# Transposes by DMA, V loads ahead of a weight load and another opening in a fused attention and mixture-of-experts kernel

## The chip, the cores and the metric

The kernel runs on one core of one Trainium2 chip. The metric is the device time of one execution in microseconds (us). The engines of a core work side by side, each through its own list of instructions in order: TensorE (PE) with its weight loads (PEld), VectorE (DVE), ScalarE (ACT), GpSimd (POOL) and SyncE (SP). Transfers are issued by SP, ACT and POOL and run on the core's 16 DMA engines.

## The reference

Attention over 32 global and 512 local tokens per batch (8 batches, 8 heads of 64), with a window of 32 to both sides for the local queries; its output is the input of a mixture of 8 experts, whose weights per token come from eight rounds of row and column scaling.

```python
out_g = sm(scale * q_g @ k_all.T) @ v_all                  # k_all = [k_g, k_l], v_all = [v_g, v_l]
s_ll  = where(|i - j| <= 32, scale * q_l @ k_l.T, -1e9)
out_l = sm([scale * q_l @ k_g.T, s_ll]) @ v_all
x = [out_g, out_l] as (B * S, H * D)                       # 4352 x 512
P = exp(x @ w_gate - max)
for _ in range(8):
    P /= P.sum(1) + 1e-9;  P /= P.sum(0) + 1e-9;  P *= N / E
out = sum over e of P[:, e] * (relu(x @ w1[e]) @ w2[e])    # w1: 512 x 1024, w2: 1024 x 512
```

## The kernel before

**Units and steps.** The attention has 32 units, n = 4b + hp: a batch b and a pair of heads hp. A loop over steps s = 0 to 33 (L453) is written out by hand, and every engine and queue keeps the written order. Step s makes the scores and probabilities of unit s and the output of unit s - 1, and does pieces of experts 0 and 1 for tokens that are ready:

- `st_A` transposes q and k of unit s + 1 on PE.
- `st_B` (in three parts, 3 + 3 + 2 blocks of 64 queries): scores on PE (L279, L281), the masked minimum on DVE (L286), exp on ACT into Pu (L289). A block of Pu is 128 local columns and 32 global ones.
- `st_D1` (unit s - 1): DVE copies the 32 global columns of all blocks to Pl (L295); PE transposes the 128 local columns of the 8 blocks (L298); DVE copies the result to pw (L300).
- `st_D2`: PE transposes xn of unit s - 2, the finished output, in four pieces (L308), and Pl of unit s - 1 (L312); ACT copies the two results to xT (L316) and to pg (L314).
- `st_E` (unit s - 1, at the end of step s): the output, from pw with va and vb (local keys) and pg with vgz (global keys), into po (L332); DVE divides into xn (L336, L337).
- `st_G1` to `st_G4`: the global queries, over the same k and V.
- `p_l1` and `p_l2` (L415, L429), called as `f1` and `f2`: four and two pieces a step of the two matrix products of experts 0 and 1, in between the parts above. They read xT, of the batch whose four units are complete. Their results go to memory (yd) by SP (L436).

Pu, pw and xn have two buffers each.

**V.** The local keys of a block of 64 queries are 128 rows that begin 32 rows before it. va holds V shifted by 32 rows, for the even blocks, and vb the rows 64 later, for the odd ones. `load_v` gives the steps of a batch's load: `first` (vg16, the global V rounded to half precision in memory, and 96 rows of va), three times `mid` (128 rows of va each) and `last`: POOL loads the final 32 rows of vb (L165), and then SP copies the rest of vb from va (L166, L167, L168) and, from batch 2 on, loads vgz from vg16 in four pieces (`load_vz`, L150).

**POOL's queue.** POOL issues every load that changes from single to half precision. At the head of a step the next entries of `queue` are taken (L466 to L474): for step 8 and later, two of the next batch's q and k loads in each of the steps hp = 0 and 1, three of its V steps at hp = 2, the rest at hp = 3. Then, in steps 8 to 31, POOL prepares weight sums that experts 2 to 7 use later (L476 to L478): an even step issues the load of a matrix (`sums_load`, tile pw, 1024 KB in half precision), the next step waits for it and forms four sums of 2.1 us each (`sums_form`, L113) and stores them (kept, L114). This tile pw has the name of the attention's pw and is another one. The V load of a batch b + 1 stands in the steps 4b + 2 and 4b + 3; its first use is the output of unit 4b + 4, in step 4b + 5.

**The opening.** Before the loop q and k of the first unit come by SP and ACT in single precision and are rounded on the core; step 0 also rounds and transposes the global q of batches 0 to 3 (`cast_g`, `transpose_g`). Steps 0 to 4 hold no expert work.

**After the loop** come the rest of experts 0 and 1 around the eight scalings (`tail`), and then experts 2 to 7 (class `Slot` and class `Unit`), from about 400 us to the end. Nothing there is edited.

Of the kernel before, what the change touches and what calls it, by code (L numbers as in the profile page):

```python
# [10 lines left out]
FP16 = mybir.dt.float16  # L11
FP32 = mybir.dt.float32
# [11 lines left out]
def kernel(  # L24
# [13 lines left out]
    nc = tc.nc  # L38

    B, H, Sl, Dh = q_l.shape  # L40
# [3 lines left out]
    P = 128  # L44
# [4 lines left out]
    NHB = Sl // HB  # L49
# [70 lines left out]
    with ExitStack() as att:  # L120
# [31 lines left out]
        def load_v(b):  # L152
            va, vb = vab[b % 2]
            vz = vgz[b % 2]
            src = v_l[b].rearrange("h s d -> s h d")

            def first():
                nc.gpsimd.dma_start(out=vg16[b], in_=v_g[b].rearrange("h g d -> g h d"))
                nc.gpsimd.dma_start(out=va[W:P, 0, :, 0:Dh], in_=src[0:96])

            def mid(j):
                nc.gpsimd.dma_start(out=va[:, j, :, 0:Dh], in_=src[P * j - W : P * j + 96])

            def last():
                nc.gpsimd.dma_start(out=vb[HB : HB + W, NJ - 1, :, 0:Dh], in_=src[Sl - W : Sl])  # L165
                nc.sync.dma_start(out=vb[96:P, NJ - 1], in_=va[W : 2 * W, 0])  # L166
                nc.sync.dma_start(out=vb[0:HB, :], in_=va[HB:P, :])  # L167
                nc.sync.dma_start(out=vb[HB:P, 0 : NJ - 1], in_=va[0:HB, 1:NJ])  # L168
                if b > 1:
                    load_vz(b)  # L170

            return [first] + [lambda j=j: mid(j) for j in range(1, NJ)] + [last]

        gst = {}

# [14 lines left out]
        def cast_g(tg):  # L190
            t, fv = gst[(0, tg)]
            nc.vector.tensor_copy(out=t, in_=fv)
            gst[(0, tg)] = t
# [72 lines left out]
        def st_B(n, part):  # L266
            b, hp = divmod(n, HP)
            qb, kt = qbd[n % 2], kTe[n % 4]
            if part == 0:
                st[n] = dict(Pu=att_wk.tile([P, NHB, SW], FP16, tag="Pu", name="Pu"),  # L270
                             mx=att_wk.tile([P, NHB], FP32, tag="mx", name="mx"))
            d = st[n]
            i0 = 3 * part
            ni = min(3, NHB - i0)
            sc = ps_sc.tile([P, 512], FP32, tag="sc")
            ms = att_wk.tile([P, 3, SW], FP32, tag="ms")
            for ii in range(ni):
                i = i0 + ii
                nc.tensor.matmul(sc[:, SW * ii : SW * ii + KW], qb[:, i, :],  # L279
                                 kt[:, HB * i : HB * i + KW], start=True, stop=True)  # L280
                nc.tensor.matmul(sc[:, SW * ii + KW : SW * (ii + 1)], qb[:, i, :],  # L281
                                 kgT[:, hp, Sg * b : Sg * (b + 1)], start=True, stop=True)
            for ii in range(ni):
                i = i0 + ii
                mi = 0 if i == 0 else (2 if i == NHB - 1 else 1)
                nc.vector.tensor_tensor_reduce(  # L286
                    out=ms[:, ii, :], in0=sc[:, SW * ii : SW * (ii + 1)], in1=mask[:, mi, :],
                    scale=-scale, scalar=BIG, op0=ALU.add, op1=ALU.min, accum_out=d["mx"][:, i : i + 1])
                nc.scalar.activation(out=d["Pu"][:, i, :], in_=ms[:, ii, :], func=AF.Exp, scale=-1.0,  # L289
                                     bias=d["mx"][:, i : i + 1])  # L290

        def st_D1(n):
            d = st[n]
            d["Pl"] = att_wk.tile([P, NHB, Sg], FP16, tag="Pl", name="Pl")
            nc.vector.tensor_copy(out=d["Pl"], in_=d["Pu"][:, :, KW:SW])  # L295
            ptw = ps_tr.tile([P, NHB, P], FP16, tag="tr")
            for i in range(NHB):
                nc.tensor.transpose(ptw[:, i, :], d["Pu"][:, i, 0:KW], identity)  # L298
            d["pw"] = att_wk.tile([P, NHB, P], FP16, tag="pw", name="pw")
            nc.vector.tensor_copy(out=d["pw"], in_=ptw)  # L300

        def st_D2(n, n2):
            tgx = ps_tr.tile([P, 6, P], FP16, tag="tr")
            if n2 is not None:
                b, hp = divmod(n2, HP)
                xn = st[n2]["xn"]
                for j in range(NJ):
                    nc.tensor.transpose(tgx[:, 2 + j, :], xn[:, j, :], identity)  # L308
            if n is not None:
                d = st[n]  # L310
                for t in range(2):
                    nc.tensor.transpose(tgx[:, t, :], d["Pl"][:, 4 * t : 4 * t + 4, :], identity)  # L312
                d["pg"] = att_wk.tile([P, 2, P], FP16, tag="pg", name="pg")
                nc.scalar.copy(out=d["pg"], in_=tgx[:, 0:2, :])  # L314
            if n2 is not None:
                nc.scalar.copy(out=xT[:, hp, Sl * b : Sl * (b + 1)], in_=tgx[:, 2:6, :].rearrange("p j q -> p (j q)"))  # L316
                del st[n2]

        def st_E(n):
            b, hp = divmod(n, HP)  # L320
            d = st[n]
            vz = vgz[b % 2]
            d["xn"] = att_wk.tile([P, NJ, P], FP16, tag="xn", name="xn")
            po = ps_po.tile([P, NJ, 256], FP32, tag="po")
            for j in range(NJ):
                for a in range(2):
                    for first in (True, False):
                        for par in range(2):
                            i, h = 2 * j + par, 2 * hp + a
                            lhs, rhs = (d["pw"][:, i], vab[b % 2][par][:, j, h, :]) if first else \  # L330
                                (d["pg"][:, i // 4], vz[:, i % 4, h, :])
                            nc.tensor.matmul(po[HB * par : HB * (par + 1), j, VW * a : VW * (a + 1)],  # L332
                                             lhs[:, HB * a : HB * (a + 1)], rhs, start=first, stop=not first)
            pv = po[:, :, 0 : 2 * VW].rearrange("p j (a v) -> p j a v", a=2)
            rr = att_wk.tile([P, NJ, 2], FP32, tag="rr2", name="rr2")
            nc.vector.reciprocal(out=rr, in_=pv[:, :, :, Dh])  # L336
            nc.vector.tensor_tensor(out=d["xn"].rearrange("p j (a v) -> p j a v", a=2), in0=pv[:, :, :, 0:Dh],  # L337
                                    in1=rr.unsqueeze(3).to_broadcast([P, NJ, 2, Dh]), op=ALU.mult)

        gs = {}  # L340

# [96 lines left out]
        def load_first():  # L438
            wts[0] = [load_w1(0)]
            nc.gpsimd.dma_start(out=wg_sb, in_=moe_w_gate.rearrange("(dko dki) e -> dki dko e", dki=P))  # L440

        queue = []
        NU = B * HP
        for t in range(2):
# [8 lines left out]
        for s in range(NU + 2):  # L453
            b, hp = divmod(s, HP)
            if s < NU and b + 1 < B:
                if hp == 0:
                    queue = load_qk(b + 1, 0, 4, H)
                if hp == 2:
                    queue += load_v(b + 1)
                if s == 4:  # L460
                    queue += [lambda: wts.__setitem__(1, [load_w1(1)]), lambda: wts[0].append(load_w2(0))]
                if s == 5:
                    queue += [lambda: load_g(1, "kgs"), lambda: load_g(1, "qgs")]
                if s == 7:
                    queue += [lambda: wts[1].append(load_w2(1))]
                take = 0 if s == 0 else len(queue) if s < 8 else 2 if hp < 2 else 3 if hp == 2 else len(queue)  # L466
                if s == 1:
                    queue += [load_first]
                    take = len(queue)
                for i, f in enumerate(queue[:take]):  # L470
                    f()
                    if s == 2 and i == 0:
                        load_vz(1)
                queue = queue[take:]  # L474
# [15 lines left out]
            def f1(eng):  # L490
                nonlocal n1
                if n1 < len(l1):
                    if l1[n1]:
                        p_l1(*l1[n1], eng)
                    n1 += 1
# [15 lines left out]
                st_G1(*divmod((s - 2) // 2, 2))  # L511
            if 1 <= s <= NU:
                st_D1(s - 1)
            if s == 3:
                st_E(1)
            if g_odd:
# [3 lines left out]
                st_B(s, 1)  # L520
            if 1 <= s:
                st_D2(s - 1 if s <= NU else None, s - 2 if s >= 4 else 0 if s == 3 else None)
            if s == 4:
                st_D2(None, 1)
            if 7 <= s < NU:
                st_B(s, 1)
            f1("a")
            if s + 1 < NU and s < 7:
                st_A(s + 1)
            if s == 0:  # L530
                cast_g("qgs")
                transpose_g(0, "qgs")
            f1("v")
            if s < NU:
# [15 lines left out]
            if s == 18:  # L550
                st_G4(0)
            f1("a")
        logits(NJ * (B - 1), NJ)


# [445 lines left out]
```

## Time and profile before

| | |
|---|---|
| three runs | 1039.04, 1041.32, 1042.68 us; median 1041.32 |
| profiled execution | 1041.35 us, its span 1039.6 us |
| busy over the span | PE 997.0, DVE 760.7, ACT 654.7, POOL 260.9 us |
| 139 to 307 us | PE 153.9, ACT 125.9, DVE 88.6, POOL 91.4 us of 168; DMA engines 92% |
| 307 to 352 us, the end of the attention loop | PE 43.5 us of 45 |
| 352 us to the end | PE 680.0 us of 687.6 |
| 128x128 transposes of Pu on PE (L298) | 256, median 0.219 us from issue to modelled end |
| 128x128 transposes of xn on PE (L308) | 128, the same |
| copy of these to pw on DVE (L300), to xT on ACT (L316) | 32 of 0.683 us, 32 of 0.605 us |
| copy of Pl on DVE (L295) | 32; shortest 0.216, median 0.222, longest 2.155 us |
| DMA queue of POOL, of SP and ACT | 87.32 MB and 50.27 MB; 47.7% and 14.9% of the 16 engines' span |

The span is the profiled stretch on the core; the execution's time has 1.75 us more around it. Busy time of PE is the time with a matrix instruction in flight, not PE at its peak. The chain that ended last is followed back from the last instruction: each piece names what released the next. A line such as "PE po L332 <- DMA vb<-va: 12.0, 3, 5.6" in the table of waits says that PE, at line 332, waited for a transfer into vb, 12.0 us in total, three times, the longest 5.6. In a timeline the columns are start, duration, engine, line, operation, output and input, and in brackets the idle time before and what ended it.

### The profile page before, as it was taken

To read this page: it belongs to the slowest core of one execution; us is meant where nothing else is said; L and a number is where in the kernel's file an instruction comes from. 1 tells how busy PE (TensorE), PEld (TensorE's weight loads), DVE (VectorE), ACT (ScalarE), POOL (GpSimd) and SP (SyncE) were. 2 spreads that over 40 slices of the span, in tenths; PEclk is the share of its full clock that TensorE was granted. 3 is DMA by queue.
4 is the path that set the end of the run, shared out by engine and by line. 5 is a ranking of instruction groups with operands and counts; after the bars stand their busy time and mean duration, and the time that the engine had idled before them with its cause. 6 is when DMAs were issued, how large, how long until landed. Compare 5 with 4: busy or idle time off the path is not lost.

```text
span 1039.6 us, 21929 instructions
## 1 busy us (share of the span) xinstructions
PE 997.0 (96%) x8650; PEld 648.6 (62%) x8650; DVE 760.7 (73%) x1862; ACT 654.7 (63%) x1377; POOL 260.9 (25%) x280
## 2 busy tenths in 40 slices
PE   5899999997979999999999999999999999999997
PEld 3666556564545554666666666676767676676764
DVE  6765565654535273689999887898889999888785
ACT  6788888876756556775555555556775555555551
POOL 7335665646463322012011111111111111011000
PEclk9899999998989999999999999999999999999999
DMA  9999988889795658465463433356554433233043
GB/s 176 193 157 165 211 142 207 147 184 169 163 195 139 189 152 243 101 165 125 111 135 87 106 60 101 76 169 183 143 133 107 105 102 90 65 72 72 1 102 122
DMA packets 134376, 139.38 MB, mean 134 GB/s; under 512 B 54144, under 2 KB 107648, under 8 KB 130688
## 3 DMA queue, kind: packets, MB, share of 16 engines
q0 software_dynamic: 103776, 87.32, 47.7%
q1 hardware_dynamic: 29664, 50.27, 14.9%
q8 instruction: 67, 1.10, 0.4%
q10 hardware_dynamic: 832, 0.39, 0.1%
q14 instruction: 37, 0.30, 0.1%
HBM read 144.20 MB, written 39.58 MB: 177 GB/s over the span
## 4 chain that ended last, share of the span: by engine, by line
PE 80%; DMA 9%; POOL 5%; DVE 2%; issue 1%; ACT 1%; SPq 1%; POOLq 0%; ACTq 0%; DVEq 0%
PE z L728 29%; PE pa L823 17%; PE pb L823 8%; PE py L429 8%; PE ph L415 7%; DMA pw<-in_moe_w_dram 5%; PE pc L823 5%; POOL psum L113 3%; DMA va<-in_v_l_dram 3%; PE zp L794 1%; PE po L332 1%; DMA vb<-va 1%; PE pt L257 1%; PE sc L279 1%; PE ptw L298 1%
## 5 line engine op out<-in xcount | busy, mean ns | idle before, releaser
L728 PEld LDWEIGHTS <-hs 128*128 128x128 f16 x2264 | 220.7, 98 | 92.9 <-issue 1.1
L728 PE MATMUL z<-w2e,hs 128*128 128x256 f16 x1304 | 195.6, 273 | 0.9 <-DVE oy L762 0.9
L728 PE MATMUL z<-v,hs 128*128 128x256 f16 x960 | 144.0, 273 | 0.0
L429 PE MATMUL py<-w2e,hT 128*128 128x512 f16 x544 | 131.5, 387 | 0.3 <-DVE lg L404 0.3
L415 PE MATMUL ph<-xT,w1e 128*128 128x512 f16 (+1 forms) x576 | 129.9, 368 | 1.8 <-DVE lg L404 1.4
L749 ACT COPY z<-z 128x256 f32<-128x256 f32 x98 | 35.0, 357 | 141.7 <-PE z L728 141.7
L823 PEld LDWEIGHTS <-w1e 128*128 128x128 f16 x960 | 86.6, 97 | 59.1 <-issue 2.5
L286 DVE CUSTOM_DVE_ANT_0 ms<-sc,mask 128x160 f32<-128x160 f32 x256 | 69.9, 320 | 69.8 <-PE sc L281 65.5
L823 PE MATMUL pa<-t,s 128*128 128x512 f16 x384 | 114.2, 379 | 0.3 <-ACT s L848 0.3
L289 ACT ACTIVATE Pu<-ms,mx 128x160 f16<-128x160 f32 x256 | 92.2, 424 | 20.5 <-DVE mx L286 18.4
L762 DVE SCALAR_TENSOR_TENSOR oy<-z,lg,oy 128x512 f32<-128x512 f32 x128 | 95.8, 749 | 7.3 <-ACT oy L767 5.1
L724 DVE TENSOR_TENSOR hs<-hs 128x512 f16<-128x512 f16 x224 | 94.8, 423 | 8.2
L827 DVE CUSTOM_DVE_ANT_0 hx<-pb,s 128x512 f16<-128x512 f32 x96 | 65.9, 686 | 40.9 <-ACT s L857 30.1
L839 ACT ACTIVATE hs<-pc 128x512 f16<-128x512 f32 x96 | 57.2, 596 | 52.5 <-PE pc L823 52.5
L415 PEld LDWEIGHTS <-w1e 128*128 128x128 f16 x576 | 54.2, 98 | 53.1 <-issue 3.8
L827 DVE CUSTOM_DVE_ANT_0 hs<-pb,s 128x512 f16<-128x512 f32 x96 | 65.8, 686 | 27.1 <-ACT s L857 26.7
L644 POOL DMA_DIRECT2D w1e<-in_moe_w_dram x24 | 17.4, 730 | 271.8 <-PE pa L823 203.4
L113 POOL TENSOR_TENSOR psum<-pw 128x1024 f16<-128x1024 f16 x24 | 50.4, 2115 | 136.8 <-DMA pw<-in_moe_w_dram 136.8
L429 PEld LDWEIGHTS <-hT 128*128 128x128 f16 x544 | 50.7, 99 | 53.8 <-issue 3.7
L823 PEld LDWEIGHTS <-s 128*128 128x128 f16 x720 | 65.6, 98 | 29.2 <-issue 0.8
L644 POOL DMA_DIRECT2D w2e<-in_moe_w_dram x24 | 19.8, 831 | 240.4 <-PE z L728 235.0
L418 ACT ACTIVATE hT<-ph 128x512 f16<-128x512 f32 (+1 forms) x115 | 63.8, 567 | 18.4 <-PE ph L415 17.6
(182 smaller groups left out, 1928.8 us busy)
## 6 DMA issues: line engine op xcount, KB each, us to landing
ys<-yd SPq DMA_DIRECT2D x68, 256.0 KB, 3.4
yd<-yst SPq DMA_DIRECT2D x16, 1024.0 KB, 5.2
pw<-in_moe_w_dram POOLq DMA_DIRECT2D x12, 1024.0 KB, 12.9
kept<-psum POOLq DMA_DIRECT2D x12, 1024.0 KB, 4.9
s<-kept POOLq DMA_DIRECT2D x12, 768.0 KB, 8.8
v<-kept POOLq DMA_DIRECT2D x12, 768.0 KB, 8.9
w1e<-in_moe_w_dram POOLq DMA_DIRECT2D x12, 512.0 KB, 5.4
w2e<-in_moe_w_dram POOLq DMA_DIRECT2D x12, 512.0 KB, 6.6
```

Source lines behind the costliest of these rows:

```text
L113: nc.gpsimd.tensor_tensor(out=o, in0=x, in1=y, op=op)
L286: nc.vector.tensor_tensor_reduce(out=ms[:, ii, :], in0=sc[:, SW * ii : SW * (ii + 1)], in1=mask[:, mi, :], scale=-scale, scalar=BIG, op0=A ...
L289: nc.scalar.activation(out=d["Pu"][:, i, :], in_=ms[:, ii, :], func=AF.Exp, scale=-1.0, bias=d["mx"][:, i : i + 1])
L415: nc.tensor.matmul(ph[:, 0:n], wts[e][0][:, dk, P * fm : P * (fm + 1)], xT[:, dk, c0 : c0 + n], start=(dk == 0), stop=(dk == DP - 1))
L418: nc.scalar.activation(out=hT[:, fm, 0:n], in_=ph[:, 0:n], func=AF.Relu)
L429: nc.tensor.matmul(py, hT[:, fk, P * c : P * (c + 1)], wts[e][1][:, fk, :], start=(fk == 0), stop=(fk == FT - 1))
L724: nc.vector.tensor_tensor(out=o, in0=x, in1=y, op=op)
L728: nc.tensor.matmul(o, lhs[:, fk, :], rhs[:, fk, :], start=(first and fk == 0), stop=(fk == HF - 1), skip_group_check=True)
L762: nc.vector.scalar_tensor_tensor(out=o, in0=z, scalar=p, in1=o, op0=ALU.mult, op1=ALU.add)
L823: nc.tensor.matmul(o, lhs[:, dk, P * f : P * (f + 1)], rhs[:, dk], start=(first and n == 0 and dk == 0), stop=(dk == HD - 1), skip_group_c ...
L827: nc.vector._custom_dve(TENSOR_ADD_SAT, out=self.to(i, j), in0=self.of(ps), in1=self.of(s), s0=BIG, s1=0.0)
L839: nc.scalar.activation(out=self.to(0, 0), in_=self.of(self.pc), func=AF.Relu)
```

## The change

- From unit 6 on the 8 local blocks of Pu are transposed by DMA, issued on SP straight after each block's exp (in `st_B`), and the finished output xn by four DMAs on SP after `st_E`, straight into xT. The PE transposes, the DVE copy to pw and the ACT copy to xT go for these 26 units. Units 0 to 5 keep them.
- The copy of the global columns to Pl is made by ACT, for all units.
- `load_v` gives its SP copies as a step of their own, `move`. All of POOL's V loads stand in step 4b + 2, ahead of that step's `sums_load`; `move` stands at the head of step 4b + 3.
- In the opening the global q is transposed in step 1, the second `st_D2` of step 4 comes after `st_A`, and steps 1 to 4 get 3 and 6 more matmuls each, into a PSUM tile that nothing reads (`keep_busy`).

```diff
             def last():
                 nc.gpsimd.dma_start(out=vb[HB : HB + W, NJ - 1, :, 0:Dh], in_=src[Sl - W : Sl])
+
+            def move():
                 nc.sync.dma_start(out=vb[96:P, NJ - 1], in_=va[W : 2 * W, 0])
                 nc.sync.dma_start(out=vb[0:HB, :], in_=va[HB:P, :])
                 nc.sync.dma_start(out=vb[HB:P, 0 : NJ - 1], in_=va[0:HB, 1:NJ])
                 if b > 1:
                     load_vz(b)
-            return [first] + [lambda j=j: mid(j) for j in range(1, NJ)] + [last]
+            return [first] + [lambda j=j: mid(j) for j in range(1, NJ)] + [last, move]
...
                 nc.scalar.activation(out=d["Pu"][:, i, :], in_=ms[:, ii, :], func=AF.Exp, scale=-1.0,
                                      bias=d["mx"][:, i : i + 1])
+                if n >= 6:
+                    if i == 0:
+                        d["pw"] = att_wk.tile([P, NHB, P], FP16, tag="pw", name="pw")
+                    nc.sync.dma_start_transpose(out=d["pw"][:, i, :], in_=d["Pu"][:, i, 0:KW])
...
-            nc.vector.tensor_copy(out=d["Pl"], in_=d["Pu"][:, :, KW:SW])
+            nc.scalar.copy(out=d["Pl"], in_=d["Pu"][:, :, KW:SW])
+            if n >= 6:
+                return
...
-            if n2 is not None:
+            if n2 is not None and n2 < 6:
...
+            if n >= 6:
+                for j in range(NJ):
+                    nc.sync.dma_start_transpose(out=xT[:, hp, Sl * b + P * j : Sl * b + P * (j + 1)], in_=d["xn"][:, j, :])
...
+        def keep_busy(n):
+            pm = ps_mm.tile([P, 512], FP32, tag="mm", name="pm")
+            for i in range(n):
+                nc.tensor.matmul(pm, identity, kgT[:, :, 0:P], start=True, stop=True)
...
                 if hp == 2:
-                    queue += load_v(b + 1)
+                    *loads, move = load_v(b + 1)
+                    queue += loads
+                if hp == 3:
+                    queue = [move] + queue
...
-                take = 0 if s == 0 else len(queue) if s < 8 else 2 if hp < 2 else 3 if hp == 2 else len(queue)
+                take = 0 if s == 0 else 2 if s >= 8 and hp < 2 else len(queue)
...
                 st_D1(s - 1)
+            if 1 <= s < 5:
+                keep_busy(3)
...
-            if s == 4:
-                st_D2(None, 1)
...
+            if s == 4:
+                st_D2(None, 1)
             if s == 0:
                 cast_g("qgs")
+            if s == 1:
                 transpose_g(0, "qgs")
...
             f1("a")
+            if 1 <= s < 5:
+                keep_busy(6)
```

More of the change, by code (lines that the diff above doesn't have):

```diff
@@ L314, in st_D2 @@
                 nc.scalar.copy(out=d["pg"], in_=tgx[:, 0:2, :])
-            if n2 is not None:
+            if n2 is not None and n2 < 6:
                 nc.scalar.copy(out=xT[:, hp, Sl * b : Sl * (b + 1)], in_=tgx[:, 2:6, :].rearrange("p j q -> p (j q)"))
```

## The prediction

> **What bounds the kernel now.** I read first the chain that ended last, as shares, then the same chain in order of time, and then the queues it passes through.
>
> ```profile
> PE 80%; DMA 9%; POOL 5%; DVE 2%; issue 1%; ACT 1%; SPq 1%; POOLq 0%; ACTq 0%; DVEq 0%
> ```
>
> TensorE (PE) holds four fifths of it, which would make every PE instruction taken away a gain. But the change touches only the attention stage, and 9% DMA with 5% POOL must lie somewhere. In order of time they lie exactly there: from 139.7 to 307 us the chain runs mostly through POOL's queue.
>
> ```profile
> 211.62 14.97 DMA pw<-in_moe_w_dram
> 226.72 4.22 POOL psum L113 x2
> ...
> 290.36 10.81 DMA va<-in_v_l_dram
> 301.30 0.51 SPq L167
> 301.87 0.59 SPq L168
> 302.55 0.58 SPq L150
> ...
> 304.67 2.27 DMA vgz<-vg
> 306.99 0.77 PE po L332 x21
> 307.75 3.53 PE py L429 x8
> ```
>
> A weight load (pw) lands, POOL forms sums for 8.5 us, then POOL issues the next batch's V loads; SP copies them to vb; only then can PE do the attention output (po, L332). POOL's own timeline shows why V comes late:
>
> ```profile
> 276.90 4.21 POOL L113 TENSOR_TENSOR psum<-pw 128x1024 f16<-128x1024 f16 x2 [13.52 <-DMA pw<-in_moe_w_dram]
> ...
> 286.38 0.60 POOL L158 DMA_DIRECT2D vg<-in_v_g_dram  x1
> 286.95 0.81 POOL L159 DMA_DIRECT2D va<-in_v_l_dram  x1
> 287.73 1.79 POOL L162 DMA_DIRECT2D va<-in_v_l_dram  x2
> 289.48 0.92 POOL L98 DMA_DIRECT2D pw<-in_moe_w_dram  x1
> 290.36 0.92 POOL L162 DMA_DIRECT2D va<-in_v_l_dram  x1
> ```
>
> The same V issues (L158) stand at 136.58, 186.24, 236.22 and 286.38: POOL needs 49.9 us for four steps. PE's own pace is 10.6 us a step (the 16 transposes ahead of st_E end, and st_E begins, at 269.57 and 280.18 in successive steps), so 42.5 us for four. POOL falls behind 7.4 us per batch. The loads of batch 7 belong to step 26; POOL makes them when PE is in step 28. PE pays at the end:
>
> ```profile
> PE po L332 <- DMA vb<-va: 12.0, 3, 5.6
> SPq L166 <- DMA va<-in_v_l_dram: 135.1, 6, 31.5
> ```
>
> The first line is all that PE waits for V. The second is what I count on most: SP already stands up to 31.5 us in front of the copies. That costs nothing now because only result stores are queued behind.
>
> **The change, part by part.** The profiled execution took 1041.35 us (span 1039.6), as good as the median of the three runs, 1041.32; the sum is made against 1041.35.
>
> Transposes off PE. 26 of 32 units lose 8 transposes of Pu (L298) and 4 of xn (L308). In the chain 8 of L298 take 0.55 or 0.46 us and 4 of L308 0.22: 0.72 us a unit, 18.7 us in all. DVE loses the copy of L300 (0.68), ACT that of L316 (0.60); both are off the chain. If PE set the pace all along, the time would fall by 18.7. It does not: whatever PE saves before step 28 only makes it wait longer for V of batch 7. After that step 3.6 us remain (three times 0.5, four times 0.22, and the 1.2 us that PE waited at 327.6 for DVE).
>
> The Pl copy to ACT (L295): on DVE it has a median of 0.22 us, a longest of 2.16. No strided ACT copy is in the trace; the same size is L314's 0.38, twice the size L316's 0.60. I take 0.38. ACT has 125.9 us of work in the 168 us from 139 to 307, and has just lost 0.60 a unit. Nothing; if ACT's queue were full, 0.38 - 0.60 a unit, a gain.
>
> V loads first. The last full piece (L162) goes ahead of pw's issue, 0.88 us earlier, and no longer behind pw in the DMA queue: it should land after the 6.8 us that the page's issue table gives such pieces, at 289.48 + 6.8 = 296.3, not 301.3. In return pw stands behind 160 KB more. Pieces and pw are 384 + 1024 KB in 13.8 us (186.81 to 200.57), so 160 KB are 1.6 us; four such cycles before 286 (V of batches 3 to 6) make POOL 6.4 us later.
>
> Moves. They stay at the start of step 4b+3, where V's tail was, but now 12 transposes a step are queued behind them on SP: those of unit 4b+3 first, whose output PE does at the end of step 4b+4. Before, the first to need the copies was unit 4b+4, a step later. So V is in effect needed one step sooner. SP's issue from L167 to the last L150 took 301.30 to 305.22, 3.9 us.
>
> The DMA transposes themselves. No row shows one. From below: a DMA issue of SP, 0.51 (L167). From above: the 2.3 us in which the smallest 32 KB copy lands (L150), if each held the queue until it landed. I take the nearest row, 32 KB copies issued one behind the other: L150, four in 2.67, so 0.67 each, and 2.7 to land. Eight: 5.3.
>
> What they take from pw. Some 25 of the 48 transposes of a cycle fall into its 26 us of pw loads, when the DMA engines show no idle time. 25 x 32 KB is 0.8 MB. From below nothing, if they find gaps; from above 4.0 us a cycle at the 200 GB/s that moved while pw loaded; at the 400 GB/s that the engines reached at 207 us, 2.0. I take 2.0, as SBUF copies had that rate: 4.5 cycles from step 8 to 26 make 9 us (0 to 18).
>
> The opening: 36 matmuls of 512 columns by 0.22 us (1.73 for 8) are 7.8 us of PE in steps 1 to 4, against a granted clock of 0.87 from 26 to 52 us. Both are covered by POOL's chain: its first pw, issued at 60.91, waited for DMA until 79.95. Without that cover a few us either way. POOL's 4.6 us at 26.6, put down to PE, ends when the first w1e, issued at 16.20 with 13.8 to land, is due: DMA again.
>
> **The sum.** Unit 27's output can start at 296.3 + 3.9 + 5.3 + 2.0 (2.7 less the last issue's 0.67) = 307.5, plus POOL's delay of 6.4 + 9 = 15.4: 322.9. One step of 10.6 - 0.7 later comes unit 28's, at 332.8, which before came at 307.0. Less 3.6 saved later: +22.2 us, **1063.6 us**.
>
> By the bounds: 0.51 an issue and no contention give 296.3 + 3.9 + 4.1 + 2.2 + 6.4 = 312.9, so +12; 18 us of contention gives +31, and a dearer issue leads over to the second case.
>
> **The rivals.** (a) The above, +12 to +31, and to +45 if sizes are worse.
>
> (b) SP becomes the bound. A step gives it 12 transposes, one quarter of the moves (4.5 / 4 = 1.1 us) and about 0.5 of stores. At 0.67 that is 9.6 us, under the 12.5 of POOL's pace. From 0.88 us an issue SP alone ends later than (a). For it: it is near already. Against: SP issues at 0.5 to 0.7 in every row. I take 1.0, just past that point, as the rows lie below it: 13.6 us x 26 units from 49 us, where step 6 begins, end at 403 where the last transposes ended at 347: +56, **1097 us**. Held until landing, 2.3 us, they would give 29 us a step and +461; SP's rows show it issuing the next DMA long before the last has landed, so I leave that end out of the range. The Trainium skill, "VectorE: DVE Perf Modes", section "The three transpose paths", gives 1309 ns for one 128x128 transpose by DMA; taken as time per issue that would be 17.3 us a step and some +155 us, 1196; no row here shows it.
>
> (c) Faster. POOL's chain gets shorter, so V is no longer late, and what PE saves counts. It decides from unit 27's output before 300.7 (307.0 + 3.6 - 9.9), that is from pw loads 0.8 us shorter each than now instead of longer (POOL 6.8 us early instead of 15.4 late, over 9 loads). At 2 us shorter each, POOL is 18 early: 289.5, so -11, **1030 us**. For it: a Pl copy of 2.07 us, at 202.87, ran beside POOL's sums, so the two engines hinder each other and DVE's copies go; V no longer straddles pw. Against: nothing leaves the DMA queues, and L113 takes 2.10 to 2.13 everywhere, so POOL is not what suffers.
>
> (d) The terms cancel: within 3 us.
>
> **How the numbers follow.** (a) 0.54, (b) 0.17, (c) 0.23, (d) 0.06. The time is that of (a), 1064. (a) alone reaches from 1048 to 1086. The range goes from 1026, where most of (c) is inside, to 1110, with the milder half of (b); some 0.18 stays out. Faster by over 0.3% (3.1 us, about what this measurement can tell) 0.23, within 0.06, slower 0.71.
>
> **What would show it.** In the new profile: SP waiting at L166 or L167 with transposes behind; PE waiting at L332 in step 4b+4 for pw from a DMA, not for vb, some 9 us each for batches 5 to 7; V issues (L158's line) spaced over 49.9 us; pw over 11 and 15 us to land; an issue time per transpose near 0.67. I am wrong in the sign if V issues come at 50 us or less and PE does not wait in step 28; wrong in the mechanism if SP is busy issuing without a wait (b), or if the stage from 352 us on changes, where nothing is edited.

## The result, and the profile after

The changed kernel takes 1244.02 us (1243.23 to 1244.38, four runs) against 1041.26 for the kernel before beside it: a ratio of 1.1966, 95% interval 1.194 to 1.1991. It is 203 us slower, where 22 were forecast, and outside the range. The profiled execution took 1243.72 us, its span 1241.9.

The chain that ended last, as shares, on the page of the changed kernel:

```profile
PE 72%; DMA 11%; SPq 6%; ACT 6%; DVE 3%; issue 2%; ACTq 0%; DVEq 0%
PE z L752 24%; PE pa L847 14%; PE py L440 9%; DMA pw<-Pu 9%; PE ph L426 7%; PE pb L847 7%; PE pc L847 4%; SPq L296 3%; SPq L349 3%; ACT Pu L291 2%; DVE ms L288 1%; DMA xT<-xn 1%; PE po L340 1%; PE zp L818 1%; PE po L387 1%
```

POOL, which had 5%, is gone from it; so are the V loads of the loop. In their place stand the transposes (pw<-Pu, xT<-xn) and SP's queue in issuing them (L296, L349). What PE waits for, in the table of waits:

```profile
PE po L340 <- DMA pw<-Pu: 101.5, 52, 7.3
PE ph L426 <- DMA xT<-xn: 62.6, 7, 14.1
```

For vb only 1.3 us are left, once, at 26.7 us in the opening, ahead of the first transpose by DMA: in the loop V is not late any more, because PE is later. The cause stands in SP's timeline (start, duration, queue, line, operation, output and input, count):

```profile
254.71 5.01 SPq L349 DMA_TRANSPOSE xT<-xn  x4
259.83 11.48 SPq L296 DMA_TRANSPOSE pw<-Pu  x8
271.40 5.01 SPq L349 DMA_TRANSPOSE xT<-xn  x4
276.52 0.53 SPq L447 DMA_DIRECT2D yd<-yst  x1
277.18 13.10 SPq L296 DMA_TRANSPOSE pw<-Pu  x8
290.37 5.34 SPq L349 DMA_TRANSPOSE xT<-xn  x4
295.83 0.55 SPq L168 DMA_DIRECT2D vb<-va  x1
```

A result store takes SP 0.53 us; four transposes take 5.01, one after the other without a pause, 1.27 us from start to start. From its first transpose to its last SP needs 494.7 us: 419.1 in the 312 transposes (a mean of 1.34), 35.8 in its 54 other DMAs and its semaphore instructions, 14.8 in pauses over 0.1 us, and 25 in the short gaps of 0.04 us between one instruction and the next, which make about 0.07 for each DMA. SP is full. In the kernel before the same stretch, 53 to 347 us, is 294 us long; the difference, 201, is nearly all of the result.

PE, waiting in every step, also runs at a lower granted clock. By stretches (length, then busy time and instructions of PE, PEld, DVE, ACT and POOL, the granted clock, DMA share, GB/s):

```profile
200.00:300.00 100.00, 60.16 (x569) 31.80 (x567) 25.10 (x112) 41.18 (x95) 40.00 (x32) 0.78 0.77 141
```

PE is busy for 60 us of 100 at a clock of 0.78. Eight matmuls py take up to 3.6 us there, 1.9 in other places. As SP pauses for only 14.8 us in all, this can have lengthened little.

### The profile page after: what moved, and what is told of

Same layout as the page of the kernel before. It is cut to its first block, busy times and chain, and to the rows that moved or that the text cites. A ratio compares the mean times of both kernels' runs of the same rounds, so it can differ in the third digit from the quotient of the medians.

```text
span 1241.9 us, 22018 instructions
## 1 busy us (share of the span) xinstructions
PE 1038.9 (84%) x8374; PEld 648.9 (52%) x8374; DVE 736.0 (59%) x1804; ACT 650.2 (52%) x1383; POOL 260.7 (21%) x280
## 4 chain that ended last, share of the span: by engine, by line
PE 72%; DMA 11%; SPq 6%; ACT 6%; DVE 3%; issue 2%; ACTq 0%; DVEq 0%
PE z L752 24%; PE pa L847 14%; PE py L440 9%; DMA pw<-Pu 9%; PE ph L426 7%; PE pb L847 7%; PE pc L847 4%; SPq L296 3%; SPq L349 3%; ACT Pu L291 2%; DVE ms L288 1%; DMA xT<-xn 1%; PE po L340 1%; PE zp L818 1%; PE po L387 1%
## 5 line engine op out<-in xcount | busy, mean ns | idle before, releaser
L426 PE MATMUL ph<-xT,w1e 128*128 128x512 f16 (+1 forms) x576 | 136.7, 379 | 64.7 <-DMA xT<-xn 62.6
L440 PE MATMUL py<-w2e,hT 128*128 128x512 f16 x544 | 156.4, 441 | 0.4 <-DVE lg L415 0.3
L443 ACT COPY yst<-py 128x512 f32<-128x512 f32 x68 | 39.7, 584 | 178.1 <-PE py L440 176.3
L440 PEld LDWEIGHTS <-hT 128*128 128x128 f16 x544 | 55.4, 109 | 69.2 <-issue 29.7
L340 PEld LDWEIGHTS <-pw 128*64 128x64 f16 x512 | 28.2, 125 | 112.7 <-DMA pw<-Pu 108.5
L113 POOL TENSOR_TENSOR psum<-pw 128x1024 f16<-128x1024 f16 x24 | 50.4, 2112 | 138.7 <-DMA pw<-in_moe_w_dram 138.7
## 6 DMA issues: line engine op xcount, KB each, us to landing
pw<-in_moe_w_dram POOLq DMA_DIRECT2D x12, 1024.0 KB, 12.1
```

Of the source, the lines that this page charges most:

```text
L113: nc.gpsimd.tensor_tensor(out=o, in0=x, in1=y, op=op)
L426: nc.tensor.matmul(ph[:, 0:n], wts[e][0][:, dk, P * fm : P * (fm + 1)], xT[:, dk, c0 : c0 + n], start=(dk == 0), stop=(dk == DP - 1))
L440: nc.tensor.matmul(py, hT[:, fk, P * c : P * (c + 1)], wts[e][1][:, fk, :], start=(fk == 0), stop=(fk == FT - 1))
```

## The experiments

In all of them T1 is the theory that the time a DMA transpose holds SP sets the pace. The rivals T2 and T3 are told with the runs that test them. A time without a ratio is that of one run; runs of the kernel before lay between 1034.89 and 1045.41 us.

**1. Each half of the change alone.** All transposes on PE, the rest of the change kept:

```diff
-                if n >= 6:
+                if n >= 99:
```

(and so at each of the places that test n or n2)

> The changed kernel with its V order, Pl copy on ACT and opening, but every transpose on PE again. Theory T1 (each DMA transpose holds SP for about 1.27 us, twelve a step are 15.2 us against PE's 10.6): nearly all of the +203 us goes, 1035 to 1050 us. Rival T2 (V order and the moves at the head of SP's queue, with the opening, carry a fifth or more of the loss): over 1080 us. By the terms of the prediction alone (V at 296.3, POOL 6.4 us later, Pl 1.2 us saved) it is within 5 us of before.

Measured: 1043.32 us, ratio 1.0039 (1.0023 to 1.0054). And the kernel before with the transposes only:

```diff
+                if n >= 6:
+                    if i == 0:
+                        d["pw"] = att_wk.tile([P, NHB, P], FP16, tag="pw", name="pw")
+                    nc.sync.dma_start_transpose(out=d["pw"][:, i, :], in_=d["Pu"][:, i, 0:KW])
...
+            if n >= 6:
+                for j in range(NJ):
+                    nc.sync.dma_start_transpose(out=xT[:, hp, Sl * b + P * j : Sl * b + P * (j + 1)], in_=d["xn"][:, j, :])
```

> The kernel before with the DMA transposes of units 6 to 31 and nothing else: V loads straddle pw as before, Pl copied by DVE, old opening. T1: 1230 to 1255 us, since V is no longer what comes late. T2: clearly under 1200 us, as the rest of the change would hold the missing part.

Measured: 1242.41 us. So the transposes are the loss; V's order, Pl on ACT and the opening together cost 2.4 to 5.6 us, by the interval of the first ratio. T2 falls. The first of the two kernels also tests the forecast's terms for V. Its chain in order of time and SP's timeline:

```profile
296.25 6.16 DMA va<-in_v_l_dram
...
299.58 0.55 SPq L168 DMA_DIRECT2D vb<-va  x1
302.55 0.51 SPq L169 DMA_DIRECT2D vb<-va  x1
```

The last large V piece lands 6.16 us after its issue (6.8 was taken), not 10.8 as before. But batch 7's V loads begin at 293.14 us instead of 286.38: POOL is 6.8 us later, for which 6.4 was worked out. SP copies at 302.55 (L169, the former L167), before at 301.30. What V won in the DMA queue it lost in POOL's, and PE's waits for vb hardly change, 10.6 us against 12.0.

That 6.8 and 6.4 agree is in part luck. The forecast had 1.6 us in each of four cycles. By the V issues of batches 3 to 7 the first cycle alone lost 6.8, the second 2.0, and the last two gained 0.6 each; the first issue was 0.8 early:

```profile
88.67 0.60 POOL L158 DMA_DIRECT2D vg<-in_v_g_dram  x1
...
142.58 0.60 POOL L158 DMA_DIRECT2D vg<-in_v_g_dram  x1
```

Before, these two stood at 89.45 and 136.58. The copy of Pl takes ACT 0.39 us, as forecast (0.38), but PE waits for it 4.8 us in all; before it waited 1.8 for DVE's.

**2. The disputed price by itself.** A kernel that is not the reference's computation: SP issues transposes and plain copies between on-chip tiles, with nothing else moving.

```python
for n, lo in ((1, 0), (2, 6), (4, 12)):
    for y in ys[lo : lo + 6]:
        nc.sync.dma_start_transpose(out=y[:, 0:n, :], in_=x[:, 0 : P * n])
for y in ys[18:24]:
    nc.sync.dma_start(out=y[:, 0, :], in_=x[:, 0:P])
```

> Not the reference's computation at all: only six transposes each of 128x128, 128x256 and 128x512 and six plain 32 KB copies between on-chip tiles, issued by SP with nothing else moving; the time of the kernel says nothing. T1: an issue takes 1.1 to 1.3 us for each of the three sizes, the plain copy 0.5. Rival T3 (the issue is slow only because the DMA engines are full): under 0.8 us each here. Price per block: 128x512 takes four times 128x128.

Its SP timeline and its DMA issues (output and input, queue, operation and count, KB, median us to landing):

```profile
3.81 23.15 SPq L37 DMA_TRANSPOSE y<-x  x18
27.01 3.81 SPq L39 DMA_DIRECT2D y<-x  x6
```

```profile
y<-x SPq DMA_TRANSPOSE x18, 2.4
y<-x SPq DMA_DIRECT2D x6, 32.0 KB, 1.8
```

Eighteen transposes in 23.15 us are 1.29 each, of which the instruction itself takes 1.24. From start to start it is 1.27 us for 128x128, 1.29 for 128x256 and 1.31 for 128x512: 128x512 costs SP what 128x128 costs. The first, with no other under way, already takes 1.19, so it is not by waiting for the transposes ahead that SP is held. A plain 32 KB copy takes 0.635. The price is per instruction, twice the row that the forecast took for it, and it needs no load on the DMA engines.

**3. Fewer instructions.** First the four transposes of xn as one:

```diff
-                for j in range(NJ):
-                    nc.sync.dma_start_transpose(out=xT[:, hp, Sl * b + P * j : Sl * b + P * (j + 1)], in_=d["xn"][:, j, :])
+                nc.sync.dma_start_transpose(out=xT[:, hp, Sl * b : Sl * (b + 1)].rearrange("p (j q) -> p j q", j=NJ),
+                                            in_=d["xn"].rearrange("p j q -> p (j q)"))
```

> The changed kernel with the four xn transposes of a unit as one DMA of 128x512, Pu as it is. If the price is per instruction, that one takes 1.2 to 1.4 us on SP, 3.8 us a step go, times 26: 1140 to 1155 us. If it is per 128x128 block, it takes about 5 us and the time stays at 1235 to 1250 us.

Measured: 1138.10 us, 2 below the range for a price per instruction: 106 less for 78 issues less, 1.36 us each. In its SP timeline the one of 128x512 takes 1.22 us:

```profile
260.44 12.13 SPq L296 DMA_TRANSPOSE pw<-Pu  x8
272.66 1.22 SPq L348 DMA_TRANSPOSE xT<-xn  x1
```

Then the blocks of Pu in pairs as well. Every second block's scores are laid out with the global columns first, so that two blocks' local columns are neighbours:

```diff
...
+                    if i % 2:
+                        f = d["Pu"].rearrange("p i w -> p (i w)")
+                        nc.sync.dma_start_transpose(out=d["pw"][:, i - 1 : i + 1, :],
+                                                    in_=f[:, SW * (i - 1) + Sg : SW * (i - 1) + Sg + 2 * KW])
```

> The changed kernel with five DMA transposes a unit instead of twelve: the scores of every second block are laid out global columns first, so that two blocks' local columns lie side by side and go as one 128x256 transpose, and xn goes as one of 128x512; Pl takes two ACT copies. T1 (an instruction holds SP for 1.27 us whatever its size): SP has 5 x 1.27 + 1.6 = 8.0 us a step, under PE's 10, so the SP bound is gone and what stays is like the kernel with xn alone: 1050 to 1080 us. Rival (the bytes or blocks on the DMA engines set the price): no better than the 1138 us of the kernel with xn in one.

Measured: 1113.52 us, above the range that T1 gave. SP is no longer full (104 us of its 362 are pauses), and still 72 us are lost. A transpose holds SP for 1.61 us here on average (median 1.22), not for the 1.27 that T1 had. PE's waits for the transposes come to nearly the loss, and the issue table tells what took SP's place:

```profile
PE ph L432 <- DMA xT<-xn: 44.7, 5, 11.5
PE po L346 <- DMA pw<-Pu: 23.0, 13, 4.7
```

```profile
pw<-in_moe_w_dram POOLq DMA_DIRECT2D x12, 1024.0 KB, 17.6
pw<-Pu SPq DMA_TRANSPOSE x104, 8.3
```

A transpose now lands after 8.3 us (2.4 when alone), and a weight load after 17.6 (12.3 in the kernel of experiment 1 without transposes). They seem to be in each other's way, which the next experiment tests.

**4. Without the weight loads.** The matrices for the weight sums are loaded once, in the changed kernel and in the one with pairs. The other eleven loads are left out, so the later sums are not those of the reference; only the time counts:

```diff
     def sums_load(e, l):
+        if "w" in work:
...
+            return
```

> The changed kernel, but the matrices for the weight sums are loaded once instead of twelve times (eleven loads of 1024 KB are left out, the sums are formed of the first). T1 (SP's issue time sets the pace): 17.2 us a step for 26 steps from 50 us, so 1180 to 1205 us; only the part that T1 leaves over of the 203 us goes. Rival T3 (the transposes wait for DMA engines that the weight loads fill): under 1130 us.

Measured: 1230.67 us. T1 was right that little goes, 13 us, but its figure of 1180 to 1205 was too low. The transposes of Pu land in 2.5 us, 3.0 in the changed kernel, and SP is as full as there: 482.2 us, 415.3 of them in the transposes and 2.7 in pauses. SP's time in issuing, not the weight loads, sets the pace of the changed kernel.

> The kernel with five DMA transposes a unit, and the matrices for the weight sums loaded once instead of twelve times (eleven loads of 1024 KB are left out, the sums are formed of the first). SP is no bound there. Theory T3 (what is left of the loss, 72 us, is transposes and weight loads in each other's way on the DMA engines): transposes land in about 2.5 us as when alone, and the time is 1030 to 1060 us. Rival (the order of the steps leaves too little time for any transpose by DMA): PE's waits for pw and xT stay, 1085 us or more.

Measured: 1059.44 us, 54 below the same kernel with the loads, at the upper edge of T3's range. So with twelve issues a unit the loads hardly matter, and with five they are most of what is left. But T3 was only half right: the transposes land after 4.5 us, not after the 2.5 that it expected, and hold SP for 1.50 us on average. So the weight loads are not the only thing in their way; what else is stays open. PE's waits in this kernel:

```profile
PE po L352 <- DMA pw<-Pu: 14.2, 8, 4.1
PE ph L438 <- DMA xT<-xn: 10.0, 4, 5.1
```

The time is still 21 us above the kernel before, of which experiment 1 puts 2.4 to 5.6 on the rest of the change. What the five transposes cost by themselves is not shown: a kernel with neither transposes nor these loads was not run.

**5. Only xn.** Pu on PE again, xn by four transposes a unit:

> The changed kernel with only the finished output xn transposed by DMA (four a step), Pu on PE again. T1: SP has 4 x 1.27 + 1.6 = 6.7 us a step, under PE's 10, so the loss is nearly gone: 1035 to 1055 us. Rival T3 (the transposes load the DMA engines and slow pw and V, whoever issues them): a third of the loss stays, about 1110 us.

Measured: 1066.73 us, between the two theories and 23 above the kernel of experiment 1 without transposes. SP has 113.7 us of pauses in 303.3. PE waits for xT, about as long as what is lost:

```profile
PE ph L420 <- DMA xT<-xn: 22.2, 5, 6.9
```

The expert pieces of the next batch read xT of a batch's last unit in the middle of the next step. Four transposes one behind the other and a landing of 5.3 us are too late for that. The weight loads land after 13.8 us instead of 12.3, and batch 7's V loads are late as well, at 303.83 us against 293.14; but PE, later itself, does not wait for them.

To see whether this wait is what lies above SP's pure issue time in the changed kernel, its last unit of each batch kept xn on PE:

```diff
-            if n >= 6:
+            if n >= 6 and hp < 3:
                 for j in range(NJ):
```

> The changed kernel, but xn of the last unit of each batch (hp = 3) is transposed on PE, because the next batch of expert pieces needs it within the step, while on SP it stands behind the eight transposes of the next unit. SP loses 5.1 us in four steps. If SP's issue time alone sets the pace, that is all that goes, 26 / 4 x 5.1 = 33 us: 1205 to 1215 us. If PE's waits for xT (62.6 us) and SP's idling after them are what lies above SP's pure issue time, they go too: 1145 to 1180 us.

Measured: 1209.69 us: 34 less for 28 issues less, 1.23 us each, which is SP's issue time and no more. PE no longer waits for xT; it waits for pw instead, 127.1 us instead of 101.5. So the wait for xT is not what lies above SP's issue time.

**6. Better than both?** POOL's lateness is what the kernel before suffers from, so the V loads were put ahead of a sum, not of a load:

```diff
+                if hp == 1 and b >= 3:
+                    *loads, move = load_v(b + 1)
+                    queue += loads
...
```

> The kernel before, without any part of the change's transposes, with POOL's V loads of batches 4 to 7 one step earlier, ahead of the sums of step 4b + 1 instead of behind them; the SP copies stay at the head of step 4b + 3. If V behind POOL's sums is what PE waits for, the two waits of 5.7 us and the half clock after them go: 1022 to 1030 us. Rival (POOL waits for V's buffers and the sums come late instead): 1037 us or more.

Measured: 1053.75 us, ratio 1.0136 (1.0098 to 1.0174). This was my mistake: in step 4b + 1 the global queries of batch b - 1 still read the 32 rows of vb that L165 overwrites, so they get rows of the next batch, and PE waits for them, since the load stands before them in the order:

```profile
PE po L378 <- DMA vb<-in_v_l_dram: 23.0, 4, 10.2
```

With L165 left in step 4b + 2, ahead of the sums' load:

```diff
+                if hp == 1 and b >= 3:
+                    *loads, last, move = load_v(b + 1)
+                    queue += loads
+                if hp == 2 and b >= 3:
+                    queue = [last]
+                if hp == 3 and b >= 3:
+                    queue = [move]
...
```

> The kernel before with POOL's loads into va for batches 4 to 7 one step earlier, ahead of the sums of step 4b + 1; the one small load into vb (L165) in step 4b + 2 ahead of the sums' load, and the SP copies at the head of step 4b + 3. Here no load touches a buffer that is still read. Theory: PE's two waits of 5.7 us for V and the half clock after them go, POOL is some 6 us later with the sums, which nobody needs yet: 1022 to 1032 us. Rival (POOL's waits for free buffers, or V in the way of pw, take it back): 1036 us or more.

Measured: 1029.79 us, ratio 0.9917 (0.9885 to 0.9948). Its profile is of an execution of 1034.70 us, 5 above the median. Of PE's waits for V in the loop only this line is left there; for vb it waits 1.7 us, at 25.9 us in the opening:

```profile
PE po L334 <- DMA vgz<-vg: 4.3, 2, 4.0
```

And the same with one transpose of xn a unit, save each batch's last:

> The kernel with early V loads, and xn of the units 6 to 31 with hp < 3 as one 128x512 DMA transpose each (19 transposes), so that no transpose is needed at once. One transpose a step is 1.3 us of SP, so SP is no bound. PE saves 0.22 us times 19, 4 us. Theory: 0 to 4 us below the same kernel without the transposes. Rival T3 (a transpose slows the weight loads and POOL with them): up to 10 us above it.

Measured: 1038.34 us, ratio 0.9985 (0.996 to 1.001), so 7 us above the kernel without them by the ratios and 9 by the medians: 19 transposes that were thought not to be needed at once, and they cost more than the 0.22 us of PE that each saves. PE waits for them:

```profile
PE ph L420 <- DMA xT<-xn: 13.7, 3, 6.2
```

They land after 7.7 us (median). T3 gave this time, but not for the right reason: the weight loads are not slower for the transposes (13.2 us, 14.2 in the kernel without). The wait of 13.7 us, which the kernel without does not have, is more than the loss. The best version found has no DMA transposes.

## Why the prediction was wrong

**The step that failed** is the price of a transpose. The prediction put 0.67 us on an issue, "the nearest row, 32 KB copies issued one behind the other". The measured price is 1.29 from issue to issue alone, and 1.34 with some 0.07 of gaps in the changed kernel. The same bytes by the same queue were not the same instruction. What followed hangs on that term: at 0.67 SP had 9.6 us of work a step, under POOL's 12.5, and POOL's loads of V set the pace. The turning point was worked out as 0.88 (the prediction's own terms give 0.89), and the real price lies beyond it. Rival (b) was the right mechanism, at a chance of 0.17 and with 1.0 us an issue too cheap. That the kernel became slower, as forecast at 0.71, was mostly for another reason than the one given: V, which was to be late, kept PE waiting for only 1.3 us, in the opening.

The Trainium skill, "VectorE: DVE Perf Modes", section "The three transpose paths", has 1309 ns for a 128x128 transpose by DMA. The trace agrees with it as the time per issue, 1.29 us; the landing took 2.4 us, and the page does not say which of the two its figure is. Taken as time per issue it gave the prediction's 1196 us, 48 below what was measured; the prediction's own terms add up to +152 and 1193, not to +155.

**What (b) still lacked**, at the price measured alone: 26 steps of 12 x 1.244 + 1.6 are 430 us, SP's stretch is 494.7. The transposes themselves are 31 us dearer (419.1 against 388), the short gaps make 25, pauses 15, and the other DMAs are some 6 less than taken. Why 65 of the 312 issues took over 1.4 us, where none of the 18 alone did, stays open; without the weight loads 48 still did.

**What held.** That POOL's sums, through V, set the pace before: with V moved ahead of a sum PE's two waits of over 5 us for vb are gone, and the time falls by 0.5 to 1.2%. That V ahead of the load gains in landing about what it costs POOL, so that the rest of the change is worth nothing or a little less: a ratio of 1.0039. Not shown is that 18.7 us less work on PE would be hidden behind V: every kernel with transposes by DMA paid for them in other places.

**What never came to bear**: SP standing before V's copies with transposes behind. V was in time, as PE was late; POOL itself waited for PE to free the buffers, 114.5 us at L165. The forecast's contention, 2 us a cycle, was a guess between 0 and 4, and its reason was misread: at 207 us a store of results (yd) was under way, not copies on the chip; while these ran, from 203 to 205 us, 217 GB/s moved. Contention was small beside SP's time in the changed kernel, and it is the larger cost once there are five issues a unit. Rival (c) would have needed POOL's chain shorter by 0.8 us a load, and reckoned with 2; the loads landed after 12.1 us instead of 12.9 in the changed kernel, stretched out as it is, and POOL waited for them as long as before, 138.7 us against 136.8.

## What to carry to other kernels

An instruction that no row of the trace shows should not be priced by the row that moves the same bytes alone; if a measured figure for it exists anywhere and it crosses a turning point of the sum, the case beyond that point deserves a good part of the chance, or a small kernel that measures the price first. Multiply a queue's price per instruction by the instructions a step gives it, and compare that with the step, before asking what the engines gain. A transpose by DMA was paid by the instruction, up to 128x512, so joining blocks into one saved most of the loss; even then, beside the weight loads, it landed late, and PE's 0.06 to 0.07 us a block was cheaper here. All transposes here were issued by SP; what they cost on another queue no run shows.

## What was not expected of the hardware

- With nothing else moving, SP issued transposes of 128x128, 128x256 and 128x512 every 1.27, 1.29 and 1.31 us; a plain 32 KB copy every 0.635 us.
- Beside weight loads, transposes of 128x256 landed after 8.3 us instead of 2.4, and the loads after 17.6 instead of 12.3. With eleven of the twelve loads left out the transposes still took 4.5.
- The changed kernel's granted clock: 0.86 from 50 to 100 us and 0.78 to 0.81 in each stretch of 100 us from there to 500, where PE waited in every step, against 0.98 before from 53 to 347.
